# A softmax-attention kernel on one core: PV moved from three chunks behind to two, exponentials cut by bank at both ends, another order of the first transfers

## Chip, cores, metric

One core of a Trainium2 chip. The metric is the device time of an execution in microseconds (us), the median of several executions. "Span" is the stretch from the first to the last instruction in the trace; time minus span is about 1.7 us in every run here. All executions told of below carry the label "fast" (within 1.5% of the fastest of their kernel).

## The reference

```python
B, Hq, Hkv, Sq, Sk, D = 16, 32, 8, 288, 512, 128      # bf16 inputs, normal * 0.05

def reference(q, k, v):
    rep = Hq // Hkv                                    # four query heads share a k/v head
    k = jnp.repeat(k, rep, axis=1)
    v = jnp.repeat(v, rep, axis=1)
    scores = jnp.einsum("bhqd,bhkd->bhqk", q, k) * D ** -0.5
    p = softmax(scores, axis=-1)
    return jnp.einsum("bhqk,bhkd->bhqd", p, v)
```

## The kernel before

The four query heads that share k and v are taken together: 128 groups ("heads" in the prediction) of 1152 query rows, nine tiles of 128, against 512 keys. Scores of a group are cut into three **chunks** of 1536 columns, which is three **banks** of PSUM as the kernel divides it (its constant BANK, 512 float32 columns). Chunks are numbered through, n = 0 to 383. For each chunk TensorE computes the scores, ScalarE exponentiates them out of PSUM into `pt_sb`, and TensorE multiplies the exponentials by v: a **batch** r of PV is twelve matmuls of 129 columns (the 129th column of v is one, and gives the sum that divides the row). VectorE divides, GpSimd copies each v into the layout with that column, SyncE starts the transfers. In every sixth chunk the last 120 columns are exponentiated by a polynomial on VectorE, to relieve ScalarE. Cuts are marked `# ...`.

```python
LAG = 3                       # batch r of PV follows the scores of chunk r + LAG

def op_warm(n, w, dst):       # matmuls of zeros; their result is not used
    for x in range(n):
        emit(nc.tensor, [("s_z", 1)], lambda: nc.tensor.matmul(
            dst[:, 0:w], z_sb[:, 0:P], z_sb[:, 0:w], start=True, stop=True))

def op_s(n):                  # the scores of chunk n
    # ...
    waits = [have("k", g), have_q(g, i)]
    if n >= 2:
        waits.append(("s_e", n - 1))          # the exp of chunk n - 2 has freed the banks
    # ... one matmul for each piece of up to 512 columns

def outs(r):                  # where a batch of PV goes
    if r == NS - 1:
        return ps_s[:, (NS - 2) % 2].rearrange("p (a e) -> p a e", e=BANK)[:, :, 0:DV]
    return ps_o[:, r % 2, 0:TPC * DV].rearrange("p (a e) -> p a e", e=DV)

def op_pv(r):
    # ... one wait for a whole batch: the exp of the last chunk that any of its rows needs
    waits = [("s_vc", g + 1), ("s_e", g * NC + uses(r % NC) + 1)]
    if 2 <= r < NS - 1:
        waits.append(("s_ev", r - 1))         # the eviction of batch r - 2

def op_exp(n):
    # ...
    parts = [(0, CH)]
    if n == 0:
        # ... the first bank by itself, then
        parts = [(BANK, CH)]
    if n == NS - 1:
        parts = [(0, CH - BANK), (CH - BANK, CH)]

# SyncE's first transfers (q of group 0 comes in two parts)
first = [lambda i=i: op_q0(i) for i in range(2)]
first += [lambda: op_q(1), lambda: op_k(0, 2), lambda: op_q(2), lambda: op_v(0, None, 2, UG), lambda: op_q(3)]

# TensorE
op_warm(WARM, BANK, ps_o[:, 1])
op_kt(0, range(1), 0)
op_kt(0, range(1, NJ), 1)
op_warm(5, P, ps_s[:, 1])
for n in range(NS):
    if n == 2:
        op_warm(4, P, ps_o[:, 0])
    op_s(n)
    if shared(n):
        op_sy(n)
    if n == 2:
        op_kt(1, range(NJ), 1)
    if n >= LAG:
        op_pv(n - LAG)
for r in range(NS - LAG, NS - 1):
    op_pv(r)
# ... the last batch, the check of the sums

# ScalarE: k of group 0, k of group 1, v of groups 0 and 1, then the exponentials
op_kd(eng, 0)
# ...
op_kd(eng, 1)
op_v(0, eng, 0, 2)
```

## Time and profile before

| | before |
|---|---|
| time, median of 3 executions | 523.03 us (522.76 to 523.08) |
| span of the profiled execution | 522.5 us |
| first scores of group 1 start | 9.88 us |
| scores of the last chunk all out | 516.08 us |
| from there to the end | 6.4 us |

The prediction shows the lines of the start and of the end. Between them the kernel repeats itself, as the chain of waits (start in us, length, engine and tile) shows of the kernel before:

```profile
450.89 0.84 PE ps_o L446 x12
474.83 0.84 PE ps_o L446 x12
498.78 0.84 PE ps_o L446 x12
```

The entries are 23.94 and 23.95 us apart, 18 chunks each.

### The profile page before, as it was taken

Reading aid. Unit: us, or ns where it says so; the run is one execution under the profiler, and the core shown is the slowest. Engines: PE = TensorE matmul, PEld = TensorE weight load, DVE = VectorE, ACT = ScalarE, POOL = GpSimd, SP = SyncE. Lnnn points to the kernel's source line nnn. Section 1 sums busy time; section 2 is a strip of 40 time slices with the busy share of each in tenths; the row PEclk is TensorE's granted clock in tenths of the full one; section 3 lists DMA queues with packets and bytes.
Section 4 is the critical chain, followed back from the end, with each engine's and each line's share of the span. In section 5 each row is a group of like instructions: output and inputs, shape, how many; then the busy total and the mean of one; then the engine's idle time right before and its main releaser. Section 6 shows DMA issues by size and latency. Waiting matters only on the chain.

```text
span 522.5 us, 15279 instructions
## 1 busy us (share of the span) xinstructions
PE 510.6 (98%) x6124; PEld 395.5 (76%) x6230; DVE 363.0 (69%) x1309; ACT 513.4 (98%) x389; POOL 79.8 (15%) x135
## 2 busy tenths in 40 slices
PE   7999999999999999999999999999999999999997
PEld 4777777777777777777777777777777777777776
DVE  1767677677677677676776776767767767767765
ACT  6999999999999999999999999999999999999996
POOL 2111111111111111111111111111111111111110
PEclk9999999999999999999999999999999999999999
DMA  8999999899899999998999999999999999997212
GB/s 174 246 219 242 260 188 226 208 225 260 208 202 273 224 184 266 241 204 219 205 267 214 199 226 230 232 230 203 238 195 235 224 218 210 205 211 179 77 69 92
DMA packets 253109, 110.05 MB, mean 211 GB/s; under 512 B 219760, under 2 KB 236784, under 8 KB 253040
## 3 DMA queue, kind: packets, MB, share of 16 engines
q1 hardware_dynamic: 252480, 108.56, 96.7%
q8 instruction: 49, 0.80, 0.7%
q10 hardware_dynamic: 560, 0.52, 0.5%
q14 instruction: 20, 0.16, 0.1%
HBM read 17.04 MB, written 37.75 MB: 105 GB/s over the span
## 4 chain that ended last, share of the span: by engine, by line
PE 96%; DMA 1%; issue 1%; SPq 0%; DVE 0%
PE ps_o L446 50%; PE ps_s L409 45%; DMA qt_sb<-in_q_dram 1%; PE ps_o L420 1%; SPq L316 0%; DVE o_sb L550 0%; DVE rl_sb L540 0%; DVE o_sb L560 0%; PE ps_o L636 0%; DVE bad_sb L586 0%; DVE flag_i L705 0%; DVE bad_sb L583 0%
## 5 line engine op out<-in xcount | busy, mean ns | idle before, releaser
L481 ACT ACTIVATE pt_sb<-ps_s 128x1536 bf16<-128x1536 f32 (+2 forms) x385 | 510.9, 1444 | 1.4 <-PE ps_s L409 1.4
L446 PE MATMUL ps_o<-v_sb,pt_sb 128*128 128x129 bf16 x4596 | 322.9, 220 | 1.3 <-DVE o_sb L550 0.2
L446 PEld LDWEIGHTS ps_o<-v_sb,pt_sb 128*128 128x128 bf16 x4596 | 283.7, 98 | 49.9 <-DVE o_sb L550 0.4
L409 PE MATMUL ps_s<-qt_sb,kt_sb 128*128 128x512 bf16 (+2 forms) x1430 | 290.6, 320 | 6.4 <-DMA qt_sb<-in_q_dram 1.9
L550 DVE TENSOR_TENSOR o_sb<-ps_o,rl_sb 128x384 bf16<-128x384 f32 x383 | 212.6, 555 | 8.9
L409 PEld LDWEIGHTS ps_s<-qt_sb,kt_sb 128*128 128x128 bf16 x1536 | 124.0, 98 | 63.5 <-ACT pt_sb L481 2.2
L540 DVE RECIPROCAL rl_sb<-ps_o 128x3 f32<-128x3 f32 x383 | 68.5, 179 | 137.0 <-PE ps_o L446 137.0
L533 POOL COPY v_sb<-vd_sb 128x512 bf16<-128x512 bf16 x128 | 78.8, 616 | 430.5 <-PE ps_o L446 416.2
L514 DVE SCALAR_TENSOR_TENSOR u_sb<-u_sb,m_sb 128x120 f32<-128x120 f32 x124 | 34.5, 278 | 0.0
L521 DVE SCALAR_TENSOR_TENSOR pt_sb<-u_sb,e_sb 128x120 bf16<-128x120 f32 x62 | 17.5, 283 | 2.1
L514 DVE SCALAR_TENSOR_TENSOR u_sb<-m_sb 128x120 f32<-128x120 f32 x62 | 17.2, 277 | 0.0
L492 DVE TENSOR_SCALAR y_sb<-ps_o 128x120 f32<-128x120 f32 x62 | 15.7, 253 | 0.0
L505 DVE TENSOR_SCALAR m_sb<-t_sb 128x120 int32<-128x120 int32 x62 | 13.8, 223 | 2.1
L505 DVE TENSOR_SCALAR e_sb<-t_sb 128x120 int32<-128x120 int32 x62 | 13.4, 217 | 0.0
L420 PE MATMUL ps_o<-qt_sb,kt_sb 128*128 128x120 bf16 x62 | 13.4, 216 | 0.0
L498 DVE TENSOR_SCALAR t_sb<-y_sb 128x120 int32<-128x120 f32 x62 | 13.2, 213 | 0.0
L420 PEld LDWEIGHTS ps_o<-qt_sb,kt_sb 128*128 128x128 bf16 x62 | 6.1, 98 | 7.3
L385 DVE COPY kt_sb<-ps_o 128x128 bf16<-128x128 bf16 (+2 forms) x3 | 1.0, 336 | 6.2 <-PE ps_o L378 6.1
L391 PE MATMUL ps_o<-z_sb 128*128 128x512 bf16 (+1 forms) x9 | 2.7, 447 | 1.3 <-DVE z_sb L667 1.3
L578 DVE TENSOR_REDUCE st_sb<-rl_sb 128x1 f32<-128x72 f32 (+1 forms) x16 | 3.5, 216 | 0.0
L576 DVE TENSOR_REDUCE st_sb<-rl_sb 128x1 f32<-128x72 f32 (+1 forms) x16 | 3.4, 215 | 0.0
L475 ACT ACTIVATE pt_sb<-ps_s 128x512 bf16<-128x512 f32 x1 | 0.6, 597 | 2.3 <-PE ps_s L409 2.3
(31 smaller groups left out, 11.0 us busy)
## 6 DMA issues: line engine op xcount, KB each, us to landing
out_dram<-o_sb SPq DMA_DIRECT2D x127, 288.0 KB, 3.5
vd_sb<-in_v_dram SPq DMA_DIRECT2D x31, 512.0 KB, 5.3
qt_sb<-in_q_dram SPq DMA_TRANSPOSE x129, 4.7
kt_sb<-in_k_dram SPq DMA_TRANSPOSE x32, 5.4
out_dram<-o_sb SPq DMA_DIRECT2D x3, 96.0 KB, 1.6
kd_sb<-in_k_dram ACTq DMA_DIRECT2D x2, 128.0 KB, 2.7
vd_sb<-in_v_dram ACTq DMA_DIRECT2D x1, 256.0 KB, 6.0
vd_sb<-in_v_dram SPq DMA_DIRECT2D x1, 256.0 KB, 3.1
```

Source lines behind the costliest of these rows:

```text
L409: ins = emit(eng, w_x, lambda: eng.matmul(ps_s[:, n % 2, c:c + w], kt_sb[:, sl, j, gi, :], qg[:, t * P:t * P + w], start=True, stop=True))
L420: emit(eng, [("s_ev", n - LAG - 1)], lambda: eng.matmul(ps_o[:, (n - LAG) % 2, BANK - W:BANK], kt_sb[:, (g // UG) % NSLOT, j, g % UG, :], ...
L446: ins = emit(eng, w_x, lambda: eng.matmul(outs(r)[:, a, :], pt(g, t, j), v_sb[:, sl, gi * NJ + j, 0:DV], start=(j == 0 and a == 0), stop=( ...
L481: emit(eng, waits, lambda: eng.activation(d, s, ACTF.Exp, scale=scale)).then_inc(sem["s_e"], 1)
L492: emit(eng, [("s_yb", nth(n) - NB), ("s_pv", n - LAG + 1)], lambda: eng.tensor_scalar(out=y_sb[:, b], in0=ps_o[:, (n - LAG) % 2, BANK - W: ...
L498: emit(eng, [("s_ym", 2 * (nth(n) - NB)), ("s_y", nth(n))], lambda: eng.tensor_scalar(out=t_sb[:, b], in0=y_sb[:, b], scalar1=Y_MUL, scala ...
L505: emit(eng, [("s_yp", nth(n) - NB), ("s_yb", nth(n))], lambda: eng.tensor_scalar(out=dst[:, b], in0=t_sb[:, b], scalar1=mask, scalar2=bits ...
L514: lambda: eng.scalar_tensor_tensor(out=u_sb[:, b, x], in0=src, scalar=QUARTIC[x], in1=m, op0=ALU.add, op1=ALU.mult)
L521: lambda: eng.scalar_tensor_tensor(out=pt_sb[:, n % NPT, CH - W:CH], in0=u_sb[:, b, 2], scalar=QUARTIC[3], in1=e_sb[:, b].bitcast(FP32), o ...
L533: emit(eng, waits, lambda: eng.tensor_copy(v_sb[:, sl, gi * NJ:(gi + 1) * NJ, 0:D], vd_sb[:, sl, gi].rearrange("p (j d) -> p j d", d=D))). ...
L540: emit(eng, [("s_pv", r + 1)], lambda: eng.reciprocal(rl_sb[:, TPC * r:TPC * (r + 1)].unsqueeze(2), outs(r)[:, :, D:DV])).then_inc(sem["s_ ...
L550: emit(eng, waits, lambda: eng.tensor_tensor(out=o_sb[:, g % NO, t0:t0 + TPC, :], in0=outs(r)[:, :, 0:D], in1=rl_sb[:, TPC * r:TPC * (r + ...
```

## The change

Its intent is to shorten both ends. Batches of PV come two chunks behind the scores, so that three and not four are left at the end; to make this possible, each PV matmul waits only for the exponentials of its own chunk (or bank). The first two chunks and the last are exponentiated bank by bank. The last two batches are built in score banks, which need no eviction first. Dummy matmuls use constants that are there from the beginning, so nothing waits for a memset (the first, before, waited for VectorE's memset until 1.27), and seven of them are dropped. The v of group 0 alone goes ahead of k of group 1 on ScalarE's queue. VectorE's last two polynomial steps come before an eviction instead of after it. GpSimd's copy of v waits for one batch of PV more than before; with the shorter lag that batch comes after the scores of the same chunk as before.

```diff
-    LAG = 3
+    LAG = 2
+    FIRST = 2
...
+        def ready(n, x):
+            if n < FIRST and x < TPC - 1:
+                return ("s_eb", n * (TPC - 1) + x + 1)
+            return ("s_e", n + 1 + (x if n == NS - 1 else 0))
...
         def op_warm(n, w, dst):
-                emit(nc.tensor, [("s_z", 1)], lambda: nc.tensor.matmul(
-                    dst[:, 0:w], z_sb[:, 0:P], z_sb[:, 0:w], start=True, stop=True))
+                nc.tensor.matmul(dst[:, 0:w], nc.const_aps.tensor(1.0, [P, P], BF16),
+                                 nc.const_aps.tensor(1.0, [P, w], BF16), start=True, stop=True)
...
         def outs(r):
             if r == NS - 1:
-                return ps_s[:, (NS - 2) % 2].rearrange("p (a e) -> p a e", e=BANK)[:, :, 0:DV]
+                return ps_s[:].rearrange("p h (a e) -> p (h a) e", e=BANK)[:, 1:1 + TPC, 0:DV]
+            if r == NS - 2:
+                return ps_s[:, 0, 0:TPC * DV].rearrange("p (a e) -> p a e", e=DV)
...
         def op_pv(r):
-            waits = [("s_vc", g + 1), ("s_e", g * NC + uses(r % NC) + 1)]
-            if 2 <= r < NS - 1:
+            waits = [("s_vc", g + 1)]
+            if 2 <= r < NS - 2:
                 waits.append(("s_ev", r - 1))
+            if r == NS - 2:
+                waits.append(("s_e", NS - 1))
...
+            todo = sequence(r % NC)          # matmuls on earlier chunks first
+            for x, (t, j) in enumerate(todo):
+                i, c = place(t, j)
+                w_x = (waits if x == 0 else []) + [ready(g * NC + i, c // BANK)]
...
         def op_exp(n):
-            if n == 0:
-                emit(eng, [("s_s0", 1)], lambda: eng.activation(d[:, 0:BANK], s[:, 0:BANK], ACTF.Exp, scale=scale))
-                parts = [(BANK, CH)]
-            if n == NS - 1:
-                parts = [(0, CH - BANK), (CH - BANK, CH)]
+            if n < FIRST or n == NS - 1:
+                parts = [(x, x + BANK) for x in range(0, CH, BANK)]
...
         def op_vc(g):
-                waits.append(("s_pv", NC * (g - 2) + 1))
+                waits.append(("s_pv", NC * (g - 2) + 2))
...
-        first += [lambda: op_q(1), lambda: op_k(0, 2), lambda: op_q(2), lambda: op_v(0, None, 2, UG), lambda: op_q(3)]
+        first += [lambda: op_q(1), lambda: op_k(0, 2), lambda: op_v(0, None, 1, UG), lambda: op_q(2), lambda: op_q(3)]
...
         def _(eng):                          # TensorE
             op_warm(WARM, BANK, ps_o[:, 1])
+            op_warm(1, P, ps_o[:, 1])
             op_kt(0, range(1), 0)
             op_kt(0, range(1, NJ), 1)
-            op_warm(5, P, ps_s[:, 1])
+            op_warm(1, P, ps_s[:, 1])
             for n in range(NS):
-                if n == 2:
-                    op_warm(4, P, ps_o[:, 0])
                 op_s(n)
...
-            for r in range(NS - LAG, NS - 1):
-                op_pv(r)
-            for a in range(TPC):
-                op_pv_last(a)
+            op_pv(NS - 2)
+            op_pv_last()
...
         def _(eng):                          # ScalarE
+            op_v(0, eng, 0, 1)
             op_kd(eng, 1)
-            op_v(0, eng, 0, 2)
...
         def _(eng):                          # VectorE
                 if shared(n - 1):
                     op_yu(n - 1, 1)
+                    op_yu(n - 1, 2)
+                    op_yp(n - 1)
                 op_ev(r)
...
-                if shared(n - 1):
-                    op_yu(n - 1, 2)
-                    op_yp(n - 1)
```

Left out: the last stores and which semaphores they count on, and the bank-wise waits of the scores of chunks 2 and 3.

## The prediction

> **What bounds the kernel now.** I read the page first: the busy shares, then the chain of waits.
>
> ```profile
> PE 510.6 (98%) x6124; PEld 395.5 (76%) x6230; DVE 363.0 (69%) x1309; ACT 513.4 (98%) x389; POOL 79.8 (15%) x135
> ...
> PE 96%; DMA 1%; issue 1%; SPq 0%; DVE 0%
> ```
>
> Two engines stand at 98%. Shares can't say which leads, so I read the timeline of a steady stretch for who follows whom.
>
> ```profile
> 252.00 0.82 PE L409 MATMUL ps_s<-qt_sb,kt_sb 128*128 128x512 bf16 x6
> ...
> 252.66 0.84 PE L446 MATMUL ps_o<-v_sb,pt_sb 128*128 128x129 bf16 x12
> ...
> 253.34 0.76 PE L409 MATMUL ps_s<-qt_sb,kt_sb 128*128 128x512 bf16 x3
> ...
> 253.99 0.84 PE L446 MATMUL ps_o<-v_sb,pt_sb 128*128 128x129 bf16 x12
> ```
>
> Start to start, the scores of a chunk take 252.66 - 252.00 = 0.66 us when four of the six pieces are narrow, about 0.65 when three are 512 wide (253.99 - 253.34), and a batch of twelve PV matmuls 253.34 - 252.66 = 0.68, or 0.0567 each. A head of three chunks costs 0.66 + 2 x 0.65 + 3 x 0.68 = 4.00 us. The chain shows batches at 43.78 and 67.73: 23.95 us for 18 chunks, 3.99 a head. TensorE is full: nothing that leaves its matmuls alone can shorten the middle. ScalarE is not far behind: one exp ends 254.36 (start 251.55, two in 2.81), the next, 120 columns shorter, 255.60. Full ones end 1.34 apart, so six chunks cost it about 5 x 1.342 + 1.243 = 7.95 us against TensorE's 7.98. (The 120 columns' 0.10 gives 0.83 ns a column, and so 0.06 us an instruction besides; used below.)
>
> What can be won is at the two ends.
>
> ```profile
> 5.31 0.10 PEld L409 LDWEIGHTS ps_s<-qt_sb,kt_sb 128*128 128x128 bf16 x1 [0.40 <-DMA qt_sb<-in_q_dram]
> ...
> 6.94 0.83 PE L409 MATMUL ps_s<-qt_sb,kt_sb 128*128 128x512 bf16 x6
> 7.61 0.39 PE L378 MATMUL ps_o<-ident,kd_sb 128*128 128x128 bf16 x4
> 9.88 0.81 PE L409 MATMUL ps_s<-qt_sb,kt_sb 128*128 128x512 bf16 x3 [1.89 <-DMA qt_sb<-in_q_dram]
> ```
>
> At the start TensorE stands idle for 1.9 us until head 1's q lands at 9.74 (the chain has that transfer: 3.51 plus 6.23). Whatever happens earlier, slow clock included, is hidden behind it.
>
> ```profile
> 516.08 1.52 PE L446 MATMUL ps_o<-v_sb,pt_sb 128*128 128x129 bf16 x24
> ...
> 517.79 0.85 PE L446 MATMUL ps_o<-v_sb,pt_sb 128*128 128x129 bf16 x12 [0.19 <-DVE o_sb L550]
> ...
> 518.48 0.84 PE L457 MATMUL ps_s<-v_sb,pt_sb 128*128 128x129 bf16 x12
> 519.37 0.17 DVE L540 RECIPROCAL rl_sb<-ps_s 128x3 f32<-128x3 f32 x1
> ```
>
> At the end four PV batches follow the last scores (whose last matmul is out at 516.08), the third waiting for an eviction until 517.79 though the second was out at 516.08 + 24 x 0.0567 = 517.44.
>
> [...] the first 512-wide matmuls start 0.43 us apart, and full rate comes about 6.2 us in. [...] q of head 1 needs 6.2 us with two heads of v and one of k in flight, others 3.0 to 4.7.
>
> **The change part by part.** I number chunks n, three to a head; batch r of PV comes after the scores of chunk r + 3 before and r + 2 after.
>
> 1. Lag 2, waits by matmul. No matmul is removed. One batch moves from behind the q wait to before it, and only three batches are left after the last scores instead of four. The price: batches 0 and 1 of each head use the chunk just being exponentiated, for their last three or four matmuls. The tightest case is the exp that started 252.88 and ended 254.36, just before the shortened one. A wait is served about 0.05 us after its exp's end (exp of chunk 0 ended 5.86 + 1.02 = 6.88, the released weight load came at 6.94): 254.41. The PV group at 253.99 would reach its ninth matmul at 253.99 + 8 x 0.0567 = 254.44. It fits by 0.03 us; the other cases of the cycle have 0.07 to 0.14. So a cost of zero in the middle, narrowly.
>
> 2. VectorE's order: two polynomial steps now precede one eviction in six chunks. Steps that depend on each other start 0.31 apart, so that eviction moves from 256.63 to about 257.27, ends 257.83, and is needed at 257.98. It fits by 0.1 us. Cost zero.
>
> 3. Start. v of group 0 alone (128 KB instead of 256) goes first on ScalarE's queue, then k of group 1; the other three v go on SyncE's queue behind q of head 1 and k. Ahead of q's landing lie 128 KB less. In the first 14 us the view of transfers has a mean of 173 GB/s: 0.75 us for 128 KB if all of it counts, but q shares its time with other traffic; I take 0.45 and have head 1's scores start at 9.43 instead of 9.88. Group 0's v lands about where group 1's k did (6.17), is copied in 0.61 by 6.85, so its PV batch goes at about 7.7 to 8.4, inside the idle stretch. Group 1's k, now second, I put at 7.6 to 8.3, plus 0.9 for transposes and copy: up to 9.2, just under q. Exp by bank, the earlier warm-up (TensorE needs no memset: 0.4 us sooner) and seven dummy matmuls fewer make chunks 0 to 2 earlier by 0.4 to 0.8 us, which q hides: worth nothing by themselves. Start: 0.45.
>
> 4. End. The moved batch saves 0.68 and the wait for the eviction 0.35 (517.79 - 517.44), since the last two batches go to score banks. In their place comes a wait for the last exp. Without the start's shift: chunk 382's exp ends about 516.51 (the last chunk's 512 part ends 517.92, less its 1024 part's 0.915 and 0.49). Cut in three, the last exp ends its banks 0.49 apart, at 517.00, 517.49 and 517.98, the last 0.06 later than now. TensorE: the scores are out at 516.08, batch 381 by 516.76, eight matmuls of 382 by 517.21, two on bank 0 by 517.33, two on bank 1 only from 517.54 to 517.65, eight of 383 by 518.11, its last four by 518.33. Now the last batch's twelfth matmul is out at 518.48 + 0.68 = 519.16: 0.83 won.
>
> 5. The finish. Reciprocal, split eviction and store follow as now. SyncE waits for most earlier stores ahead of its last issues, so about two of its waits (0.07 to 0.09 each) no longer follow the last landing: 0.16.
>
> Sum: 0.45 + 0.83 + 0.16 = 1.44 us, 0.28%. 523.03 - 1.44 = 521.6.
>
> **The rivals.**
> (a) The narrow wait becomes real. If the ninth matmul comes late by 0.03 us in each six chunks, ScalarE starts that much later next time and the delay comes back: 64 x 0.03 = 1.9 us lost, time 523.5. For it: the margin of 0.03. Against it: the cycle repeats to a few ns over the run, and the waiting weight loads at 6.94 and 517.79 had their matmuls start within 0.01 us. I give it 15%.
> (b) A new transfer binds at the start. Heads 1 to 3's v land as one transfer behind q and k: by bytes about where q of head 2 landed before (11.36), plus 0.67 for wait and copy: 12.0, against a need at about 12.7. Or group 1's k comes later than q. Either costs up to 0.7, so only 0.7 to 1.0 is won: 522.2. 30%.
> (c) q lands as soon as its bytes allow (0.75, or more as the early clock and exp by bank no longer stand behind it): 521.0 to 521.2. 25%.
> (d) q's transfer is bound by itself, not by v: start worth 0, time 522.0.
>
> **Range and chances.** The end is sure within 0.3, the start worth -0.3 to +1.0, with (a) as a tail upward: 521.6, eight in ten from 520.7 to 522.6. Two per cent is 10.5 us, more than both ends hold in idle time, and nothing that I found costs as much: faster 0.005, within 2% 0.985, slower 0.01.
>
> **What would show it.** Right: TensorE's busy time stays within 1 us of 510, the steady period 23.95 for 18 chunks; the q wait shrinks with a PV batch before it; no PV wait on VectorE at the end, the last PV out about 1.3 earlier. Wrong: weight loads waiting for exp in every sixth chunk (a), a PV wait on the v copy near 12 us (b), head 1's scores still at 9.88 (d). If the period grows by even 0.1 us in 18 chunks, the middle, not the ends, decides, and the sum above falls.

What the traces showed: the first 512-wide matmuls 0.43 us apart, full rate about 6.2 us in, 6.2 us for q of head 1. The sum: 0.45 (start) + 0.83 (last batches) + 0.16 (finish) = 1.44 us, 523.03 - 1.44 = 521.6. That head 1's q would come 0.45 us sooner with 128 KB less ahead of it was the estimate, from the 173 GB/s of the first 14 us.

## More of the kernel before

A thing that I passed over: the profiled execution itself took 524.22 us, 1.2 us more than the median of the timed ones. The trace that the prediction reads is of an execution slower than most.

## The result and the profile after

The changed kernel took 522.83 us (median of four: 523.58, 522.30, 522.20, 523.36), the kernel before in the same rounds 523.06 us. The ratio is 0.9995, with a 95% interval from 0.9977 to 1.0014. (Ratios here are the mean time of one kernel's fast runs over that of the other's of the same rounds, so not quite the ratio of the medians.) 522.83 lies above the predicted range of 520.7 to 522.6.

The four times stand in two pairs, 1.2 us apart. The profiled execution (span 521.9, time 523.58) is one of the upper pair. So I repeated both kernels unchanged, to have a profile of the lower group of the new kernel and of an ordinary execution of the old one. These two runs, e1 and e2 below, are used here already.

| us | before, as the prediction read it | before, again (e2) | after (upper group) | after, again (e1, lower group) |
|---|---|---|---|---|
| second part of group 0's q lands | 5.27 | 5.70 | 6.53 | 6.56 |
| q of group 1 lands | 9.74 | 8.59 | 7.99 | 7.93 |
| TensorE steps to its full clock (the trace's record) | 6.17 | 6.15 | 9.64 | 5.25 |
| first scores of group 1 start | 9.88 | 8.72 | 10.35 | 8.92 |
| from there to the last scores out | 506.20 | 506.20 | 506.22 | 506.26 |
| from there to the end | 6.4 | 6.4 | 5.3 | 5.3 |
| span | 522.5 | 521.3 | 521.9 | 520.5 |

**The middle.** 506.20 became 506.22 and 506.26 us. The page of the changed kernel, its engines' busy line and the shares of its chain of waits, and then three entries of that chain:

```profile
PE 517.0 (99%) x6223; PEld 395.2 (76%) x6223; DVE 368.2 (71%) x1307; ACT 513.7 (98%) x393; POOL 79.8 (15%) x135
...
ACT 97%; PE 1%; DMA 1%; issue 1%; DVE 0%; SPq 0%
```

```profile
462.23 7.93 ACT pt_sb L514 x6
470.21 7.93 ACT pt_sb L514 x6
478.19 7.93 ACT pt_sb L514 x6
```

The chain now names ScalarE where it named TensorE. That looks like a change of the bound, and is none: six chunks are 7.98 us apart here, and 18 were 23.95 before, which is 7.98 for six. The two engines were equally full, and which one an inferred chain follows is then a matter of hundredths. The busy time of TensorE rose from 510.6 to 517.0 us though seven matmuls fewer are issued: matmul records are missing from the trace of before (the count of recorded score matmuls is 1430 against 1536), so busy time says nothing here.

**The end.** The timeline of TensorE after the last scores, which are out at 516.57, in the changed kernel (start, length, engine, line, operation and tiles, count):

```profile
516.57 0.84 PE L477 MATMUL ps_o<-v_sb,pt_sb 128*128 128x129 bf16 x12
517.25 0.62 PE L477 MATMUL ps_s<-v_sb,pt_sb 128*128 128x129 bf16 x8
518.02 0.40 PE L477 MATMUL ps_s<-v_sb,pt_sb 128*128 128x129 bf16 x4
518.25 0.84 PE L490 MATMUL ps_s<-v_sb,pt_sb 128*128 128x129 bf16 x12
```

Three batches follow instead of four, the middle one goes to a score bank, and no wait for an eviction is left. A wait for the last exponentials has come in, as the prediction expected: eight matmuls are out 8 x 0.0567 after 517.25, at 517.70, and the next four start at 518.02. The last batch starts 518.25 - 516.57 = 1.68 us after the last scores are out; it was 518.48 - 516.08 = 2.40 before. From the last scores to the end it is 5.32 to 5.36 us instead of 6.40.

**The start.** Here is what was given back. TensorE's timeline in the profiled execution of the changed kernel (upper group), then in e1 (lower group), then of the kernel before in e2:

```profile
3.79 1.44 PE L437 MATMUL ps_s<-qt_sb,kt_sb 128*128 128x512 bf16 x3
6.57 2.74 PE L437 MATMUL ps_s<-qt_sb,kt_sb 128*128 128x512 bf16 x9 [1.34 <-DMA qt_sb<-in_q_dram]
...
10.35 0.81 PE L437 MATMUL ps_s<-qt_sb,kt_sb 128*128 128x512 bf16 x3
```

```profile
3.77 1.44 PE L437 MATMUL ps_s<-qt_sb,kt_sb 128*128 128x512 bf16 x3
6.61 1.48 PE L437 MATMUL ps_s<-qt_sb,kt_sb 128*128 128x512 bf16 x9 [1.40 <-DMA qt_sb<-in_q_dram]
...
8.92 0.81 PE L437 MATMUL ps_s<-qt_sb,kt_sb 128*128 128x512 bf16 x3
```

```profile
4.34 2.41 PE L409 MATMUL ps_s<-qt_sb,kt_sb 128*128 128x512 bf16 x6
6.58 0.39 PE L391 MATMUL ps_o<-z_sb 128*128 128x128 bf16 x4
6.94 0.83 PE L409 MATMUL ps_s<-qt_sb,kt_sb 128*128 128x512 bf16 x6
...
8.72 0.81 PE L409 MATMUL ps_s<-qt_sb,kt_sb 128*128 128x512 bf16 x3 [0.73 <-DMA qt_sb<-in_q_dram]
```

The first two are cut at two groups that lie between (transposes and a PV batch), the third at one (transposes). Three readings. First, an ordinary execution of the kernel before waits 0.73 us for q of group 1, not the 1.89 that the prediction had before it. Second, in the new kernel nothing waits for q of group 1 any more; TensorE stands idle earlier, for 1.34 to 1.40 us, until the *second part of group 0's q* lands at 6.5. Third, the same nine score matmuls then take 1.48 us in e1 and 2.74 us in the profiled execution of after, though q came at the same time: TensorE is on half its clock. (The trace records two states of the clock, full, 1.00, and half: 0.50 and 0.51 granted from 10.6 to 14.0 us in e14 and e4. Before the step to full the starts of the 512-wide matmuls lie 0.43 us apart, after it 0.65 / 3 = 0.22, by the lines that the prediction shows.)

### The profile page after: what moved, and what is told of

Same layout as the page of the kernel before. It is cut to its first block, busy times and chain, and to the rows that moved or that the text cites. A ratio compares the mean times of both kernels' runs of the same rounds, so it can differ in the third digit from the quotient of the medians.

```text
span 521.9 us, 15338 instructions
## 1 busy us (share of the span) xinstructions
PE 517.0 (99%) x6223; PEld 395.2 (76%) x6223; DVE 368.2 (71%) x1307; ACT 513.7 (98%) x393; POOL 79.8 (15%) x135
## 4 chain that ended last, share of the span: by engine, by line
ACT 97%; PE 1%; DMA 1%; issue 1%; DVE 0%; SPq 0%
ACT pt_sb L514 96%; DMA qt_sb<-in_q_dram 1%; PE ps_s L437 1%; SPq L316 0%; ACT pt_sb L509 0%; PE ps_o L477 0%; DVE o_sb L583 0%; PE ps_o L404 0%; DVE o_sb L593 0%; PE ps_s L477 0%; DVE rl_sb L573 0%; PE ps_o L667 0%; DVE bad_sb L619 0%; DVE flag_i L733 0%; DVE bad_sb L616 0%
## 5 line engine op out<-in xcount | busy, mean ns | idle before, releaser
L437 PE MATMUL ps_s<-qt_sb,kt_sb 128*128 128x512 bf16 (+2 forms) x1536 | 310.9, 325 | 1.3 <-DMA qt_sb<-in_q_dram 1.3
L509 ACT ACTIVATE pt_sb<-ps_s 128x512 bf16<-128x512 f32 x6 | 3.3, 627 | 2.9 <-PE ps_s L437 2.9
L417 PE MATMUL ps_o<-const-bfloat16-1.0 128*128 128x512 bf16 (+1 forms) x6 | 2.4, 573 | 0.9 <-PEq L751 0.9
```

Source lines behind the costliest of these rows:

```text
L437: ins = emit(eng, w_x, lambda: eng.matmul(ps_s[:, n % 2, c:c + w], kt_sb[:, sl, j, gi, :], qg[:, t * P:t * P + w], start=True, stop=True))
```

## The experiments

Four series; the runs of a series were on one chip and share the executions of the kernel before. Each diff below is against the changed kernel unless it says otherwise.

### e1_after_again: the changed kernel, no edit

> The changed kernel once more, for the spread of its executions and a second profile. What I now think (theory H): its executions fall into two groups, about 1.2 us apart in span (the four known ones are 520.5, 520.5, 521.7, 521.9), by whether the second part of head 0's q comes at about 5.5 us or a microsecond later, since in the late case TensorE stands idle for over 2 us[...]. Then a profile in the lower group shows q by about 5.6, full clock by about 6.2, head 1's scores before 9.2, and a profile in the upper group repeats 6.5, 9.6 and 10.3. Rival R1: the two groups come from the end (the last stores' landing), then the start looks the same in both. Rival R2: they come from the middle, then the distance from head 1's scores to the last scores differs from the 505.6 us that both profiles have.

Measured: 522.22 us (522.11 to 523.79), before 522.94; ratio 0.9992 (0.9979 to 1.0006). Spans 520.5, 520.4, 520.5, 520.4, and 522.1. With the four first executions (521.9, 520.5, 520.5, 521.7) that is six executions at 520.4 to 520.5 and three at 521.7 to 522.1. The two groups are real, and the median of four happened to fall between them.

### e2_before_again: the kernel before, no edit

> The kernel before as a run of its own, so that the span of each execution is on record. Its one profile (span 522.5) went with a time of 524.22, above its other times (523.03). If it too has two groups (theory H says that its wait for head 1's q hides the clock's step, so its groups, if any, come from q of head 1 landing earlier or later): spans of 521.2 to 521.4 in most executions, time minus span of about 1.7. If it has one group: all spans within 0.3 us of each other.

Measured: 523.07 us; ratio to the before of the same rounds 1.0007 (0.9993 to 1.002), so the method has no offset to speak of. Spans 521.3, 521.3, 521.4, 522.4, 521.2. The kernel before has an upper execution now and then (spans of 522.4 and 522.8, and one of 522.0, among the 45 of the four series, besides the first profile), and the trace that I predicted from was one.

### e3_old_dma: the first transfers in the order of before, all else changed

```diff
-        first += [lambda: op_q(1), lambda: op_k(0, 2), lambda: op_v(0, None, 1, UG), lambda: op_q(2), lambda: op_q(3)]
+        first += [lambda: op_q(1), lambda: op_k(0, 2), lambda: op_q(2), lambda: op_v(0, None, 2, UG), lambda: op_q(3)]
...
-            op_v(0, eng, 0, 1)
             op_kd(eng, 1)
+            op_v(0, eng, 0, 2)
```

> The changed kernel with only the order of the first transfers as before (ScalarE: k of group 1, then v of groups 0 and 1; SyncE: q of head 2 ahead of the other v). If the new order is what delays the second part of head 0's q (the new order's fault), q comes by 5.3, full clock at about 6.2 and there is one group. But the first PV batch then waits for v that lands at 9.5 or so and holds head 1's scores to about 10.9 (9.56 + 0.05 + 0.61 copy + 0.68 batch), so the span should be 521.4 to 522.0. If the order has nothing to do with it, the two groups stay.

Measured: 521.86 us (521.79 to 522.19); ratio 0.9981 (0.9967 to 0.9994). Spans 520.0 to 520.5, no upper group. Group 0's second part of q lands at 5.64 instead of 6.53 and group 1's q at 8.25 instead of 7.99; group 1's scores start at 8.64, without a wait for group 1's q:

```profile
5.69 2.03 PE L437 MATMUL ps_s<-qt_sb,kt_sb 128*128 128x512 bf16 x9 [0.48 <-DMA qt_sb<-in_q_dram]
...
8.64 0.81 PE L437 MATMUL ps_s<-qt_sb,kt_sb 128*128 128x512 bf16 x3
```

So the new order of transfers, which I had credited with 0.45 us, brings group 1's q 0.3 us sooner, which nothing waits for, and group 0's 0.9 us later, which TensorE waits for. The other profiles agree on group 0's second part of q: it lands at 5.27 to 6.03 in all nine with the old order (before, e2, e3, e7, e8, e9, e11, e12, e13) and at 6.53 to 6.68 with the new one (after, e1, e6, e10; at 5.85 in e5, where ScalarE's transfers began later). Whether the new order costs time in the lower group isn't shown: group 1's scores start at 8.92 in e1 and 8.82 in e10, at 8.64 here, but at 8.89 and 8.98 in e9 and e12, which have the old order too.

### e4_hold_v: ScalarE's second and third transfer wait for group 0's q

```diff
             for (s, n) in need(eng, [("s_kd0", 16)]):
                 eng.wait_ge(s, n)
+            for (s, n) in need(eng, [("s_qp1", 16)]):
+                eng.wait_ge(s, n)
             op_v(0, eng, 0, 1)
```

> The changed kernel, with ScalarE's transfers of v of group 0 and k of group 1 held until the second part of head 0's q has landed. Theory H with contention as the cause of the late q: q lands by 5.0 to 5.3 in each execution, full clock by 6.2, one group; v and k come later (7.8 and 8.5), head 1's scores at about 9.3, span 520.7 to 521.2 in each execution. If q's landing is late by itself (the transposes', not the contention's, doing), the two groups stay, 1.2 us apart.

Measured: 526.95 us; ratio 1.0077 (1.0063 to 1.0091). The q of group 0 did come, at 5.05, and group 1's at 6.94, the earliest of all runs. But k of group 1 was now issued at 5.51, with SyncE's 384 KB of v close behind (6.25), and landed at 10.59, over 5 us later; TensorE stood idle for it and lost its clock (at 10.66). A miss for the time; for the cause it says that the transfers which ScalarE starts early do delay q (one profile). What the clock did is used below.

### e5_fill_wait: dummy matmuls in the idle stretch

```diff
                 op_s(n)
+                if n == 0:
+                    op_warm(4, BANK, ps_o[:, 1])
```

> The changed kernel with four 512-wide dummy matmuls on constants added after chunk 0's scores, so that TensorE stays busy while the second part of head 0's q is awaited (6.5 us in both profiles of the changed kernel). If the slower group of its executions (span 521.7 to 522.1 against 520.4 to 520.5) is the clock's step[...], no execution of this one is in it: all spans within 0.4 us, at 520.3 to 520.8. If the slower group comes from something else (transfers), one execution in three stays about 1.2 us above the rest.

Measured: 522.36 us (521.88 to 523.03); ratio 0.9984 (0.9971 to 0.9997); spans 521.3, 520.4, 521.3, 520.7, 520.2. Inconclusive. The spread remained, and the profile fell on an execution whose first transfers were late for another reason (first part of q at 4.69); there the dummies themselves ran until 7.4 us, when q had been there since 5.85. The clock did step at 7.16 in it, not at 9.64 as in after, and the nine score matmuls took 1.46 us, at full clock; yet this execution is 1.1 us above the fastest of the run. So late transfers, here with the fill, can make an execution as slow as a missed step does. A fill of fixed length is paid for when the wait is short.

### e6_k_first: k of group 1 ahead of v on ScalarE's queue

```diff
-            op_v(0, eng, 0, 1)
             op_kd(eng, 1)
+            op_v(0, eng, 0, 1)
```

> The changed kernel with one swap: ScalarE issues k of group 1 ahead of v of group 0 (both 128 KB), SyncE's order as changed. In the changed order the last few of the sixteen increments of the second part of head 0's q come at 6.4 to 6.6; in the old one all by 5.7. If v before k is what does it, q is back at 5.7, head 1's scores start by 8.4, span about 519.9 to 520.2. If it is that a second transfer of only 128 KB gets into the engines sooner than the 256 KB one did, q stays at 6.5 and the spans at 520.4 with some at 521.7.

Measured: 523.60 us; ratio 0.9999 (0.9986 to 1.0012); spans 522.2, 520.4, 520.4, 521.8, 522.4, 522.0, four of six in the upper group. Second part of q at 6.55, as in after. The order of the two on ScalarE's queue isn't what makes q late.

### e7_lag3: PV three chunks behind again, on top of e3

```diff
-    LAG = 2
+    LAG = 3
...
-            op_pv(NS - 2)
+            for r in range(NS - LAG, NS - 1):
+                op_pv(r)
```

> The variant with the old order of first transfers (span 520.15) with the lag back at three chunks. My working has the lag worth one PV batch (0.68 us) at the end: four batches after the last scores again. At the start head 1's scores no longer stand behind a PV batch and can go at about 8.3 to 8.4 instead of 8.64. Net 0.35 to 0.5 slower: 520.5 to 520.65. Rival: the lag is worth nothing since ScalarE's last exp bounds the end anyway (exp of the last chunk is out 0.06 plus 1.40 after that of the one before): then 519.9, faster by the start's 0.3.

Measured: 535.19 us; ratio 1.0227 (1.0207 to 1.0248), the only run outside 2%. This is 13 us, and they are in the middle: in the wait table of this run one kind of wait was served 62 times, 0.5 us each. TensorE's weight load, VectorE's polynomial step and GpSimd's copy in one stretch of this run:

```profile
PEld ps_o L477 <- DVE o_sb L583: 31.5, 62, 0.5
```

```profile
255.68 0.68 PEld L477 LDWEIGHTS ps_o<-v_sb,pt_sb 128*128 128x128 bf16 x12 [0.51 <-DVE o_sb L583]
```

```profile
253.95 0.89 DVE L547 SCALAR_TENSOR_TENSOR u_sb<-u_sb,m_sb 128x120 f32<-128x120 f32 x2
```

```profile
253.75 0.65 POOL L566 COPY v_sb<-vd_sb 128x512 bf16<-128x512 bf16 x1 [3.38 <-PE ps_o L477]
```

The same two steps in e3, where no copy lies beside them:

```profile
255.19 0.60 DVE L547 SCALAR_TENSOR_TENSOR u_sb<-u_sb,m_sb 128x120 f32<-128x120 f32 x2
```

Two polynomial steps take 0.89 us together instead of 0.60. The first of them began at 253.95, while GpSimd's copy ran (253.75 to 254.39), and ended at 254.52, 0.13 us after the copy; it took 0.57, the second 0.28. With the polynomial now ahead of the eviction, the eviction comes that much later, and the PV batch waits for it. So it is over the whole run: the 62 of these steps that began while GpSimd copied took 0.57 us each, the other 62 took 0.28. By what way the copy lengthens the step isn't shown. This run combined the old lag with the changed moment of GpSimd's copy, so it isn't a clean test of the lag; e11 is.

### e8_end_in_ps_o: batch 382 back in its own bank, behind the eviction, on top of e3

```diff
-            if r == NS - 2:
-                return ps_s[:, 0, 0:TPC * DV].rearrange("p (a e) -> p a e", e=DV)
...
-            if 2 <= r < NS - 2:
+            if 2 <= r < NS - 1:
                 waits.append(("s_ev", r - 1))
-            if r == NS - 2:
-                waits.append(("s_e", NS - 1))
```

> The variant with the old order of first transfers, with the last batch but one back in its usual bank, behind the eviction of two batches earlier. My prediction put 0.35 us of the end on moving it. But with lag 2 that eviction is over at 516.89 in the profile of the changed kernel, before the batch's first matmul at 517.25, so I now expect no difference: span 520.15 within 0.1. If the prediction's step is right in itself, 520.5.

Measured: 522.10 us; ratio 0.9987 (0.9974 to 1.0); spans 521.4, 520.2, 522.5, 520.4, 520.4, 520.4. The lower group, 520.2 to 520.4, is that of e3: the score bank for batch 382 is worth nothing once the lag is two. (Its timeline shows why: twenty PV matmuls go in one stretch from 516.16, without a wait for the eviction, and the next four start at 517.61, 1.45 us after the last scores, as they do in after.) And two of six are upper ones although the transfers have the old order. The profile fell on one of these (below).

### e9_early_old and e10_early_new: chunk 1 begins with what the first part of q allows

```diff
                 if n == 0 and x < 2:
                     w_x = [("s_k0", 1), waits[1]] if x == 0 else waits[:1]
+                if n == 1 and x < 2:
+                    w_x = [waits[0], ("s_qp0", 16)] if x == 0 else waits[1:2]
```

e9 has this on top of e3 (old order of transfers), e10 on the changed kernel (new order).

> The variant with the old order of first transfers, and chunk 1's first 512 scores, which need only the first part of head 0's q, no longer held for the second part. Theory H (the clock's step is lost when TensorE idles about 5 to 6.5 us): idle time there shrinks from 0.5 to 0.9 us to nearly nothing, so the slower group goes: all spans 520.0 to 520.5, where the same variant without this edit gave 520.0 to 520.5 and, with the end's edit, 521.4 and 522.5 in two of six. If one execution in three stays 1 us above the rest, it isn't TensorE's idling that makes the groups.

> The same edit on the changed kernel itself (new order of first transfers, second part of q at 6.5). Idle time in the critical stretch falls from 1.5 to about 1.1 us, so theory H expects the slower group to remain but to be rarer or as often, and the faster group at 520.1 to 520.4 (0.2 at most better: the matmul runs in time that was idle).

Measured: e9 522.18 us (521.97 to 522.34) against 523.20, ratio 0.9978 (0.9965 to 0.9991), spans 520.3 to 520.6, no upper group. e10 522.06 us, ratio 0.9987 (0.9973 to 1.0), spans 520.4, 520.3, 520.4, 521.9, 520.3, 521.7: two of six in the upper group. The earlier piece shortens the idle stretch a little (0.83 us in e9), but the start of group 1's scores, 8.89, isn't earlier than in e3 (8.64): in e9 a batch of PV now waits for the copy of v.

```profile
5.83 1.26 PE L439 MATMUL ps_s<-qt_sb,kt_sb 128*128 128x512 bf16 x8 [0.83 <-DMA qt_sb<-in_q_dram]
...
8.20 0.85 PE L479 MATMUL ps_o<-v_sb,pt_sb 128*128 128x129 bf16 x12 [0.89 <-POOL v_sb L568]
8.89 0.81 PE L439 MATMUL ps_s<-qt_sb,kt_sb 128*128 128x512 bf16 x3
```

Under the old order, where v of two groups is one transfer, this is the next bound of the start. The new order of transfers removes it (no wait for the copy of v in after and e1).

### e11_lag3_vc1: e7, with GpSimd's copy at its old moment

```diff
-                waits.append(("s_pv", NC * (g - 2) + 2))
+                waits.append(("s_pv", NC * (g - 2) + 1))
```

> Lag three again with the old order of transfers, and GpSimd's copy of v released one batch earlier, as the kernel before had it, so that it no longer falls onto VectorE's polynomial (in the lag-3 run one step took 0.57 us instead of 0.28 while GpSimd copied, the eviction behind it came late and TensorE waited 0.5 us in every sixth chunk: 13 us). If that overlap is the whole of the 13 us, the middle is back (23.95 us for 18 chunks) and the span is 520.5 to 520.7, lag 2 being worth 0.4 to 0.5 us. If VectorE's new order alone is to blame, most of the 13 us stays.

Measured: 522.73 us; ratio 0.9992 (0.998 to 1.0004). The middle is back at 506.2, so the overlap with GpSimd's copy accounted for all of e7's loss. From the last scores to the end it is 5.72 us, against 5.34 or so with lag two and 6.40 before. So of the 1.06 us won at the end, the lag is worth about 0.4 on top of the other parts, which alone (e11) win 6.40 - 5.72 = 0.68. Spans 520.6, 520.5, 521.5, 520.5, 521.7, 521.8.

### e12_first0: no exponentials by bank at the start, on top of e3

```diff
-    FIRST = 2
+    FIRST = 0
```

> The variant with the old order of first transfers, with chunks 0 and 1 exponentiated whole (not by bank). My prediction called exp by bank at the start worth nothing. Exp of chunk 1 then ends at about 8.1, that of chunk 2 at 9.5 instead of 9.2; TensorE's scores of chunk 4 come at about 9.9 and find it done. Expected: no difference, 520.0 to 520.5 in the faster group. If exp by bank matters, 0.3 to 0.4 more.

Measured: 522.19 us; ratio 0.9981 (0.9968 to 0.9994), the same as e3; one execution of five at 521.3, the others 520.2 to 520.6. The exponentials by bank at the start are worth nothing that shows in the time, as predicted.

### e13_start_before: the whole start as before, the end as changed

e12, with the memset of zeros and all the dummy matmuls of before:

```diff
-            op_warm(1, P, ps_o[:, 1])
             op_kt(0, range(1), 0)
             op_kt(0, range(1, NJ), 1)
-            op_warm(1, P, ps_s[:, 1])
+            op_warm(5, P, ps_s[:, 1])
             for n in range(NS):
+                if n == 2:
+                    op_warm(4, P, ps_o[:, 0])
                 op_s(n)
```

> The changed kernel with its start as before: warm-up on a zeroed tile with the old fourteen dummy matmuls, old order of first transfers, chunks 0 and 1 exponentiated whole; lag, waits by matmul, VectorE's order and the end as changed. If the end's part of my sum holds (1.04 us between the last scores and the end, kernel before 6.40, changed 5.36) and the start is where the rest went: full clock always by 6.2 as in both profiles of the kernel before, one group, span 0.9 to 1.2 below the kernel before's (521.2 to 521.4) in nearly all executions. If slower executions (1.2 above) are as frequent as in the changed kernel (6 of 15 or so), the dummy matmuls that were taken away do not make them.

Measured: 521.98 us (521.82 to 522.29) against 522.87; ratio 0.9983 (0.9969 to 0.9996). Spans 520.6, 520.2, 520.2, 520.1, 520.6: one group, 0.9 us below the median of before in the same series, 521.1. With the old start, the changed end gives about what was predicted of it (0.99). The start is not wholly that of before: chunk 0 is exponentiated whole, and with lag two a batch of PV stands ahead of group 1's scores, which start at 9.03 in the profile (8.72 in e2). From the last scores on it is the changed kernel's end.

### e14_hold_k: of ScalarE's early transfers only v, k held back until group 0's q is there

e10, with one wait more:

```diff
             op_v(0, eng, 0, 1)
+            for (s, n) in need(eng, [("s_qp1", 16)]):
+                eng.wait_ge(s, n)
             op_kd(eng, 1)
```

> The changed kernel with chunk 1's first 512 scores released early, and k of group 1 issued only when the second part of head 0's q has landed. If the second 128 KB transfer of ScalarE's queue is what makes the last increments of that q come at 6.4 to 6.7, they come by 5.7 now, as in the old order; TensorE's idle stretch is under 0.5 us and no execution is in the slower group; k lands at about 7.3, head 1's scores start at 8.3 to 8.6 and the span is 0.3 to 0.6 below the best so far: 519.8 to 520.2. If q stays at 6.5, it's the first transfer (v at 5.5) that delays it, and slower executions stay.

Measured: 526.31 us; ratio 1.0064 (1.005 to 1.0077). A miss: with only v under way on ScalarE's queue nine of the sixteen completions of group 0's second part of q still came at 6.04 to 6.39, and k, held back, was issued at 6.42 beside SyncE's v and landed at 10.57, late as in e4. TensorE stood idle 1.75 us for it and lost the clock (at 10.63). Against e4, where v too was held and q was there at 5.05, v alone is enough to delay q (one profile of each; e14 has also the early piece of e10). Why q comes sooner in the old order, where k goes first and a longer v follows, stays open: e6 has k first too and q at 6.55, and e3 and e6 differ in the size of ScalarE's v and in where SyncE's v stands.

### What the record of the clock shows over all runs

The trace records when TensorE's clock is granted in full. In e4 and e14 it was on for 6.83 us (3.83 to 10.66; 3.80 to 10.63) and then at half for 3.41 (to 14.07; 14.04). So I asked of each profile how busy TensorE was in the 3.41 us that ended at a recorded step, and in the neighbouring 3.41 us, where no step came. The cut into such stretches is mine; what the chip itself goes by isn't in the trace. The columns are the stretch, its length, then busy time with the number of instructions for TensorE, its weight loads, VectorE, ScalarE and GpSimd, granted clock, transfers' share and GB/s. (The clock column reads 1.00 before the first recorded step whatever the clock is, so the pace of the matmuls has to be looked at.) First after, then e1:

```profile
2.82:6.23 3.41, 2.41 (x10) 0.72 (x8) 0.58 (x2) 1.57 (x3) 0.61 (x1) 1.00 0.79 165
6.23:9.64 3.41, 3.07 (x14) 1.69 (x15) 0.00 (x0) 1.86 (x4) 0.00 (x0) 1.00 1.08 233
```

```profile
1.84:5.25 3.41, 3.37 (x13) 1.06 (x10) 0.58 (x2) 1.74 (x4) 0.00 (x0) 1.00 0.76 189
```

Then e6 and e8, the two other profiles of upper executions, and e4, which had the full clock at 3.83 and lost it at 10.66:

```profile
3.40:6.81 3.41, 2.07 (x8) 0.54 (x7) 0.58 (x2) 1.57 (x3) 0.00 (x0) 1.00 0.90 188
```

```profile
2.71:6.12 3.41, 2.59 (x12) 0.83 (x10) 0.58 (x2) 1.60 (x4) 0.00 (x0) 1.00 0.81 190
```

```profile
3.83:7.24 3.41, 2.18 (x8) 0.49 (x8) 0.26 (x1) 1.18 (x3) 0.00 (x0) 1.00 0.85 166
7.24:10.65 3.41, 0.76 (x6) 0.30 (x7) 0.00 (x0) 3.21 (x5) 0.61 (x1) 1.00 1.09 197
```

| stretch that ended | TensorE busy, of 3.41 us, and run |
|---|---|
| with the step to full clock | 2.88 (e10), 2.94 (e14), 2.97 (e4), 2.98 (e11), 3.01 (e5), 3.07 (after, second stretch), 3.16 (e13), 3.18 (e12), 3.29 (e9), 3.37 (e1), 3.41 (before, e2, and the second stretches of e6 and e8) |
| without it, clock still half | 2.07 (e6), 2.41 (after), 2.59 (e8) |
| clock full and kept | 1.77 (e14), 2.07 (e10), 2.18 (e4), 2.28 (e12), 2.33 (e9) |
| clock full and lost | 0.76 (e4), 1.18 (e14); at the end of the run, after the last work, 1.55 (e9), 1.75 (e12) and less in the others |

No stretch of the table is out of order: at half clock those with 2.88 us of work or more ended with the step, those with 2.59 or less didn't; at full clock those with 1.77 or more kept it, those with 1.75 or less lost it (1.75 is e12's last, 516.05 to 519.46; the ends of matmuls are modelled in the trace, so these two can't be told apart). That is how these fourteen profiles fall, not a limit shown for other kernels. In after TensorE was idle for 1.00 of the 3.41 us up to 6.23 (3.41 - 2.41, the larger part of the 1.34 us wait); no step came there, and it came 3.41 us later, at 9.64. (e3 has no record of a step. Its nine matmuls took 2.03 us, between the 1.48 of the full and the 2.74 of the half clock, so by estimate it stepped about 1.1 us into them, at 6.8. e7 has none either; its nine took 2.74, all at half clock, though it has the old order and waited only 0.71 us for q.)

Two executions of one kernel part here: TensorE is idle from 5.21 to 6.61 us in e1 and from 5.23 to 6.57 in after, but in e1 the step came at 5.25, when that stretch had only begun, and in after behind it, at 9.64. In the eleven profiles other than after, e6 and e8 the recorded first step lies anywhere from 3.80 (e14) to 7.16 us (e5); why it comes now sooner, now later, isn't shown. The runs e3 and e13, whose profiles have shorter idle stretches there (0.48 and 0.25 us), had no upper execution among five each; e8, with 0.82, missed the step in the profiled one.

The count over all executions fits that. Those 1.0 us or more above the fastest of their own kernel in the same series were 9 of 21 with the new order of transfers (after and e1 together, e6, e10), 6 of 27 with the old order and the dummies dropped (e3, e8, e9, e11, e12), and 2 of 50 with all dummies in place (the kernel before in the four series, e13; a third is 0.9 above). Between the first two kinds the difference may be chance; between both and the third it is hardly that, but it isn't the dummies' doing alone: 45 of the 50 are the kernel before, where the wait for group 1's q (0.73 us in e2) would cover half of what a late step cost here (10.35 - 8.92 = 1.43), and leave less than the 1.0 us counted. Only e13's five have the dummies without that cover, and none of five against e12's one of five may be chance. Of the slow executions of the first two kinds only three were profiled, all three with a missed step; that the others had one too is argued from their like times, not shown. The profiled slow executions of e5 and of the kernel before had late transfers (e5 the fill besides) and no missed step.

## Why the prediction was wrong

**"Start: 0.45" failed, in two ways.** It was worked out from a wait of 1.89 us for group 1's q, ending in scores at 9.88. That execution was an outlier: an ordinary one of the kernel before (e2) has the scores at 8.72, with a wait of 0.73. The time it was subtracted from, 523.03, was of ordinary executions. A baseline of one kind and a gain worked out from another don't belong in one sum. The transfer itself did what the step said: q of group 1 came 0.6 us sooner than in e2 (7.93 to 7.99 against 8.59). But it no longer set the start of the scores.

**The step's premise failed as well: "Whatever happens earlier, slow clock included, is hidden behind it."** It holds for the kernel before, up to the wait that there is (0.73 us in e2). In the new kernel the cover is gone just because q of group 1 came sooner, and what it covered grew: the second part of group 0's q lands at 6.5 instead of 5.3 to 5.7, and the dummies that filled TensorE are fewer. The prediction counted the seven dropped dummies as a gain that q hides, "worth nothing by themselves"; with them, and with scores that began 0.5 us later (4.34 against 3.79) and a q that came sooner, the 3.41 us up to the step were full (all 3.41 busy in before and e2). How much of that is the dummies' part was not measured by itself. The start came to 8.72 - 8.92 = 0.20 us lost in the lower group, and 8.72 - 10.35 = 1.63 us lost where the clock step was missed. The start also carries the batch of PV that lag two moves there, 0.68 us (it starts at 8.14 in e1, group 1's scores straight after it at 8.92). The prediction let it run inside the wait for q of group 1; no such wait was left. Measured by itself, the new order doesn't win its 0.45: e3 without it has 0.9981 (0.9967 to 0.9994), e1 with it 0.9992 (0.9979 to 1.0006), intervals that overlap. e3 has no upper execution, but e8, with the old order too, has two of six. Rival (d), a start worth nothing, came nearest, but by another way; none of the rivals had a start that loses. One reading of the prediction is wrong besides: of the transposed q's in the first 14 us not all others landed within 3.0 to 4.7 us; q of group 2 took 5.1 (6.29 to 11.36), and 4.7 is the median over the whole run.

**The middle was right.** Cost zero was predicted; 506.20 became 506.22 to 506.26. Rival (a), the margin of 0.03 us of the waits on the chunk just being exponentiated, fell: no such loss appears. The price of VectorE's new order was foreseen with a margin of 0.1 us, and that is thin. The wait table of the changed kernel:

```profile
PEld ps_o L477 <- DVE o_sb L583: 13.7, 62, 0.2
```

62 weight loads wait 0.22 us each for an eviction, once in six chunks, but no matmul is later for it: the page's list of lines has 0.0 us of idle time before TensorE's matmuls of that line. e7 shows what happens when another 0.3 us are added: 0.5 us of wait and 13 us of loss.

**The end was right as a sum, less so in its parts.** Predicted 0.83 + 0.16 = 0.99 us, measured 6.40 - 5.34 = 1.06, with e13 giving 0.9 by itself. TensorE's last PV matmul was out 519.16 - 516.08 = 3.08 us after the last scores in before, was predicted at 518.33 - 516.08 = 2.25, and came at 518.25 + 0.68 - 516.57 = 2.36: 0.72 won, not 0.83, since all four matmuls that wait for exponentials wait until 1.45 us after the scores, where the prediction had two of them start sooner. The finish behind it gave 1.06 - 0.72 = 0.34 instead of 0.16. And the parts of the 0.83 don't stand for themselves: the 0.35 of the score bank isn't there once the lag is two (e8), and the 0.68 of the moved batch is about 0.4 once the other parts are there (e11), since both end in the same wait for exponentials.

**Rival (b)** didn't come true in the form given: v of groups 1 to 3 landed at 10.56, before it was needed, and k of group 1 at 6.76, before q. **Rival (c)**, q sooner than its 0.45, did come true for q and brought nothing, since q was no longer what TensorE waited for.

The sum with the measured terms: in the lower group -0.20 (start) - 0.06 (middle) + 1.06 (end) = 0.80 us won, from a span of 521.3 to 520.5 (measured 520.5). In the upper group -1.63 - 0.02 + 1.06 = 0.59 lost, to 521.9 (measured 521.9). Without the upper group the time would have been 522.2, within the range and 0.6 above the number; what put the median above the range are the two upper executions of four, of which the profiled one had the missed step of the clock (the other has no profile).

**What stays open:** why ScalarE's early transfers hold back the last part of group 0's q, and why less in the old order. In e1, ten of its sixteen completions were in by 5.65 and the last six came at 6.37 to 6.56; in e3 all sixteen were in by 5.64. In e6 a single one was late, at 6.55 (the fifteen others by 5.63). In e4, with both transfers held back, all were in at 5.05. By what way the two delay it, no run here shows.

**A version that beats the kernel before.** e9 has the lowest ratio, 0.9978 (0.9965 to 0.9991), with no upper execution among five; e3 (0.9981), e12 (0.9981) and e13 (0.9983) can't be told from it. What they share is the changed end with the old order of the first transfers. That any of them beats the changed kernel is not shown: its interval in e1, 0.9979 to 1.0006, overlaps theirs, and e8, with the old order too, has 0.9987.

## What to carry to other kernels

Before a prediction, set the profiled execution's span against the timed ones: where they differ by more than what is to be won, its waits at the start are not those of the median. When a wait at the start is shortened, ask what it had been hiding, the clock of TensorE above all; dummy matmuls that look useless under such a wait may be what lets the clock step in time (in the profiles here the step came after stretches of 3.41 us with 2.88 us of work or more, and not after those with 2.59 or less). And a sum of small gains at both ends should be tested end by end, as e13 and e3 do, for one may give back what the other wins.
